# State parts by pairs, a searched order, and one transposing transfer per chunk in place of TensorE turns

## The chip, the cores and the metric

The kernel runs on one core of a Trainium2 chip. The metric is the device time of one execution in microseconds. The engines are TensorE (PE, with its weight loads as PEld), VectorE (DVE), ScalarE (ACT), GpSimd (POOL) and SyncE (SP), which only issues transfers.

## The reference

A gated linear attention over 4 batches, 8 heads, 768 tokens and heads of 48 is followed by a token and channel mixer. In NumPy, cut to what matters:

```python
f = 1.0 / (1.0 + np.exp(-f_logit))
for t in range(S):                       # state: (B, H, 48, 48)
    state = f[:, :, t, :, None] * state + einsum('bhd,bhe->bhde', k[:, :, t], v[:, :, t])
    y[:, :, t] = einsum('bhd,bhde->bhe', q[:, :, t], state)
x = y.transpose(0, 2, 1, 3).reshape(B, S, 384)
h = maximum(x.transpose(0, 2, 1) @ w_tok1, 0) @ w_tok2     # 768 -> 256 -> 768
u = x + h.transpose(0, 2, 1)
out = u + maximum(u @ w_ch1, 0) @ w_ch2                    # 384 -> 1536 -> 384
```

## The kernel before

Each batch is cut into 6 chunks of 128 tokens. For a chunk, `gates` computes the log of the gate in three ACT ops and splits it into two bfloat16 parts, `Lhi` and `Llo`. `attention` then does the following, with buffer set `i = c % 2`:

- `sums` (L350 to L353): PE sums the logs over tokens with a triangular matrix, and over the whole chunk with a vector of ones.
- ACT takes the exponentials `G` and `Gi` (L361, L363) and, for all but the last chunk, `glast` (L366). DVE makes `qh = q*G` and `kh = k*Gi` (L369, L371), each padded to 64 columns per head.
- `turn` (L382): PE transposes `qh` and `kh`, four 128x128 blocks each, into one PSUM bank; DVE copies the bank to `qkT` (L386).
- `scores` (L396): for each head a product with 48 rows on one half of the array's rows; DVE masks both banks into `AmT` (L403).
- `parts` (L419): for each head the chunk's state update from `kh` and `v`, 64 columns of the array wide, two heads of a pair one above the other in one bank. DVE adds it to the state (`tsum`, L429) and scales by `glast` (L431; chunk 0 does both in L426). ACT, or POOL in batch 3, copies the state in two halves into `state_bd`.
- `outs` (L448, L455): PE multiplies `qkT` by the state before this chunk and `AmT` by `v` into one bank, which is copied to `x_bf` and `x_nat` (L311 on ACT, L313 on DVE; ACT alone in batch 0).

`mixer` follows for each batch: tok1 (L480), tok2 (L492) with the add L496 and the copy to `u_bf` (L311), transposes (L508) to `uT` (L513), ch1 (L524) with a relu on ACT (L534) or DVE (L536), ch2 (L546) with the add L552, and the store on SP's queue (L555). Loads of weights and of q, k, v go through POOL's queue (L255, L262); the first six gate loads go through SP's.

The order is not the program's. Every step is recorded with `add`: the engines that may run it, a rank, the buffers it needs and makes, its PSUM bank and a `kind` from which `Plan.cost` has its time. `Plan.order` keeps a clock for each engine and takes, again and again, the step that can start first, with the rank deciding between equals; it also picks the engine where several are allowed, and the PSUM bank. The steps are issued in the order of their planned starts, so each engine's queue is fixed before the kernel runs, and an engine waits at the head of its queue. The lines that say the choice:

```python
t = max(t, free[e])
if op.bank is not None and op.bank.at is None:
    t = max(t, min(banks) + 55)
if best is None or (t, op.rank) < best[0]:
    best = ((t, op.rank), e, op)
```

Ranks come from due times: attention of batch 0 every 3 us a chunk, of batch 1 from 36 us every 4, of later batches from 62 us and 101 us every 5, so that attention of one batch runs between the ch1 and ch2 products of the batch before it.

Of the kernel before, what the change touches and what calls it, by code (L numbers as in the profile page):

```python
# [10 lines left out]
FP32 = mybir.dt.float32  # L11
BF16 = mybir.dt.bfloat16
# [5 lines left out]
NBANK = 8  # L18
RING = 16384

# [19 lines left out]
class Plan:  # L40
# [58 lines left out]
    def order(self):  # L99
        for op in self.ops:  # L100
            first = op.before | ({op.behind} if op.behind else set())
            op.missing = len(first)
            for x in first:
                x.after.append(op)
        free = {e: 0.0 for e in (PE, ACT, DVE, POOL, SP)}
        ready = {e: [] for e in free}
        banks = [0.0] * NBANK
        wire = 0.0
        landed: list = []
        done = []  # L110

        def offer(op):
            t = max([x.end for x in op.before], default=0.0)
            if op.kind[0] == "load" and op.engines == (POOL,) and op.kind[3]:
                if len(landed) >= 8:
                    t = max(t, landed[-8][0])
                held = op.kind[2]
                for at, rows in reversed(landed):
                    held += rows
                    if held > RING:  # L120
                        t = max(t, at)
                        break
            for e in op.engines:
                ready[e].append((t + (WAKE[e] if t else 0.0), op))

        for op in self.ops:
            if not op.missing:
                offer(op)
        while len(done) < len(self.ops):
            best = None  # L130
            for e, line in ready.items():
                for t, op in line:
                    if op.engine is not None:
                        continue
                    t = max(t, free[e])
                    if op.bank is not None and op.bank.at is None:
                        t = max(t, min(banks) + 55)
                    if best is None or (t, op.rank) < best[0]:
                        best = ((t, op.rank), e, op)
            (t, _), e, op = best  # L140
            ready[e] = [(a, o) for a, o in ready[e] if o is not op and o.engine is None]
            if op.bank is not None and op.bank.at is None:
                op.bank.at = min(range(NBANK), key=lambda j: banks[j])
                banks[op.bank.at] = math.inf
            own, till = self.cost(op, e)
            op.engine, op.start = e, t
            free[e] = t + own
            op.end = t + till
            if op.kind[0] == "load":
                size = op.kind[3]  # L150
                if size:
                    wire = max(wire, t + 1700) + size
                    op.end = wire + 1100
                if size and e == POOL:
                    landed.append((op.end, op.kind[2]))
            if op.bank is not None:
                op.bank.users -= 1
                if not op.bank.users:
                    banks[op.bank.at] = op.end
            done.append(op)  # L160
            for x in op.after:
                x.missing -= 1
                if not x.missing:
                    offer(x)
        return sorted(done, key=lambda o: o.start)
# [7 lines left out]
def kernel(  # L173
# [20 lines left out]
    NB = 3  # L194

# [22 lines left out]
    G = [st([128, H, D], BF16, f"G{i}") for i in range(2)]  # L218
    Gi = [st([128, H, D], BF16, f"Gi{i}") for i in range(2)]
    qh = [st([128, H, 64], BF16, f"qh{i}") for i in range(2)]  # L220
    kh = [st([128, H, 64], BF16, f"kh{i}") for i in range(2)]
    qkT = [st([128, 8, 128], BF16, f"qkT{i}") for i in range(2)]
    AmT = [st([128, 8, 128], BF16, f"AmT{i}") for i in range(2)]
    glast = [st([128, HP], FP32, f"glast{i}") for i in range(2)]
    state = st([128, HP, D], FP32, "state")
    tsum = st([128, HP, D], FP32, "tsum")
    state_bd = [st([128, HP, 2 * D], BF16, f"state_bd{i}") for i in range(2)]
# [54 lines left out]
    for i in range(2):  # L282
        for n, tl in (("L", Lhi[i]), ("L", Llo[i])):
            once(DVE, lambda tl=tl: nc.vector.memset(tl[:, :, :, D:64], 0.0), [("L", i, c) for c in range(NCH)], 400)
        for n, tl in (("qh", qh[i]), ("kh", kh[i])):
            once(DVE, lambda tl=tl: nc.vector.memset(tl[:, :, D:64], 0.0), [(n, i)], 120)
        once(DVE, lambda i=i: nc.vector.memset(state_bd[i], 0.0), [("sbd", i)], 220)
# [47 lines left out]
    def attention(b, c, r):  # L335
        i, nb = c % 2, b % NB
# [43 lines left out]
        def turn(src, o):  # L380
# [3 lines left out]
        add(PE, r, lambda: turn(qh[i], 0), need=["ident", ("qh", i)], bank=p_t, kind=mms(*[C] * 4))  # L384
        add(PE, r, lambda: turn(kh[i], 4), need=["ident", ("kh", i)], bank=p_t, kind=mms(*[C] * 4))
        add(DVE, r, lambda: nc.vector.tensor_copy(qkT[i], turned()), make=[("qkT", i)], bank=p_t,  # L386
            kind=("el", 1024, True, 2))
# [11 lines left out]
        add(PE, r, lambda: None, need=[("qkT", i)], bank=p_a[0], kind=("mm", 1))  # L399
        two = add(PE, r, scores, need=[("qkT", i)], bank=p_a[1], kind=("mm", 270))  # L400
# [9 lines left out]
        if not last:  # L410
            p_d = Bank()

            def dg():
                return banks[p_d.at][:, 0:HP * D].rearrange("p (hp e) -> p hp e", e=D)

            def parts():
                for h in range(H):
                    hp, par = h // 2, h % 2
                    nc.tensor.matmul(dg()[par * 64:par * 64 + 64, hp, :], lhsT=kh[i][:, h, :],  # L419
                                     rhs=v_sb[nb][:, h, c, :], start=True, stop=True)  # L420

            add(PE, r, parts, need=[("kh", i), vk], bank=p_d, kind=("mm", 210))
            gb = glast[i].unsqueeze(2).broadcast_to((128, HP, D))
            small = ("el", HP * D, True, 1)
            if c == 0:
                add(DVE, r, lambda: nc.vector.tensor_tensor(state, dg(), gb, ALU.mult),  # L426
                    need=[("glast", i)], make=["state"], bank=p_d, kind=small)
            else:
                add(DVE, r, lambda: nc.vector.tensor_tensor(tsum, state, dg(), ALU.add),  # L429
                    need=["state"], make=["tsum"], bank=p_d, kind=small)  # L430
                add(DVE, r, lambda: nc.vector.tensor_tensor(state, tsum, gb, ALU.mult),  # L431
                    need=["tsum", ("glast", i)], make=["state"], kind=small)
            for rows, cols in ((slice(0, D), slice(0, D)), (slice(64, 64 + D), slice(D, 2 * D))):
                op = add(ACT if b <= 2 else POOL, r, None, need=["state"], make=[("sbd", i, cols.start)],
# [10 lines left out]
        def before():  # L445
            yh = y().rearrange("t (h e) -> t h e", e=D)
            for hp in range(HP):
                nc.tensor.matmul(yh[:, 2 * hp:2 * hp + 2, :], lhsT=qkT[i][:, hp, :],  # L448
                                 rhs=state_bd[(c - 1) % 2][:, hp, :],
# [10 lines left out]
        j = (c - 1) % 2  # L460
# [6 lines left out]
        past = [("qkT", i), ("sbd", j), ("sbd", j, 0), ("sbd", j, D)] if c > 0 else []  # L467
        add(PE, r, outs, need=[*past, ("AmT", i, 0), ("AmT", i, 1), vk], bank=p_y,
            kind=mms(*([96] * 4 if c else []), *[48] * 8))
        for tl, key in ((x_bf[b % 2], ("x_bf", b % 2, c)), (x_nat[b % 3], ("x_nat", b % 3, c))):  # L470
            op = add(ACT if b == 0 else (ACT, DVE), r, None, make=[key], bank=p_y, kind=el)
# [144 lines left out]
```

## Time and profile before

| what | us |
|---|---|
| median of 3 runs (188.82 to 189.28) | 188.99 |
| the profiled execution, its own time | 188.64 |
| its span | 186.8 |
| first PE instruction | 6.08 |
| first ch1 product of batch 0 | 37.75 |
| end of the last ch2 product | 183.4 |

The span is the time from the first to the last instruction of the program; 1.84 us of the execution lie around it. Busy shares over the span are PE 92%, DVE 69%, ACT 68% and POOL 35%. A PE instruction's listed time includes its way through the array, and the next one starts before it ends, so what a group costs PE is the time from its start to the next group's start. The same holds for DVE and ACT, whose ops overlap by some 0.08 to 0.12 us.

### The profile page before, as it was taken

What the parts mean: (1) busy time and instruction counts of PE and PEld (TensorE: products, weight loads), DVE (VectorE), ACT (ScalarE), POOL (GpSimd) and SP (SyncE); (2) the same over time, 40 slices, a digit from 0 to 9 for tenths busy, and PEclk for the clock granted to TensorE, in tenths of its full rate; (3) what the DMA queues carried; (4) which work ended last, traced back from release to release, by engine and by line L of the source; (5) the groups of instructions that cost most, each with busy time, mean ns of one, the idle gap of its engine ahead of it and who ended that gap; (6) DMA issues with size and microseconds to landing.
All of it is one profiled execution on the core that took longest, in us unless ns stands there. A gap on an engine that the chain in (4) does not pass through costs nothing.

```text
span 186.8 us, 4480 instructions
## 1 busy us (share of the span) xinstructions
PE 172.5 (92%) x1768; PEld 109.6 (59%) x1768; DVE 129.7 (69%) x295; ACT 126.9 (68%) x309; POOL 65.9 (35%) x78
## 2 busy tenths in 40 slices
PE   0589997799999999999999999999999999999992
PEld 0256664366667656676665665766666656656650
DVE  4387985749998999999988758977686638300222
ACT  4779963779983499999999935657875116698000
POOL 7999893275791444504621411011011000000000
PEclk9999999999999999999999999999999999999998
DMA  7999999999999999999992121011000121110222
GB/s 102 140 171 154 156 208 245 186 160 194 143 135 238 174 149 172 242 200 109 83 116 14 52 78 42 0 46 44 4 0 4 55 75 40 46 42 0 81 91 84
DMA packets 88437, 19.95 MB, mean 107 GB/s; under 512 B 81152, under 2 KB 87600, under 8 KB 88416
## 3 DMA queue, kind: packets, MB, share of 16 engines
q0 software_dynamic: 78720, 13.77, 91.9%
q1 hardware_dynamic: 9696, 5.90, 10.8%
q8 instruction: 14, 0.23, 0.5%
q14 instruction: 7, 0.06, 0.1%
HBM read 25.17 MB, written 4.72 MB: 160 GB/s over the span
## 4 chain that ended last, share of the span: by engine, by line
PE 84%; ACT 6%; DVE 3%; issue 2%; DMA 2%; POOL 1%; POOLq 0%; DVEq 0%; ACTq 0%
PE ps L524 26%; PE ps L546 24%; PE ps L382 7%; PE ps L480 5%; PE ps L396 4%; PE ps L492 3%; PE ps L455 3%; PE ps L419 3%; PE ps L352 2%; PE ps L508 2%; PE ps L353 2%; DMA f_sb<-in_f_logit_dram 2%; PE ps L448 2%; ACT u_bf L311 2%; ACT x_bf L311 1%
## 5 line engine op out<-in xcount | busy, mean ns | idle before, releaser
L546 PE MATMUL ps<-w_ch,zT 128*128 128x384 bf16 x288 | 54.1, 327 | 0.0
L524 PE MATMUL ps<-uT,w_ch 128*128 128x384 bf16 x288 | 52.6, 327 | 0.0
L534 ACT ACTIVATE zT<-ps 128x384 bf16<-128x384 f32 x76 | 36.5, 490 | 8.3 <-PE ps L524 7.9
L546 PEld LDWEIGHTS <-zT 128*128 128x128 bf16 x288 | 26.8, 98 | 16.5
L524 PEld LDWEIGHTS <-w_ch 128*128 128x128 bf16 x288 | 26.3, 97 | 15.9
L403 DVE TENSOR_TENSOR AmT<-ps,tri_bf 128x512 bf16<-128x512 f32 x48 | 30.6, 683 | 5.2 <-PE ps L396 5.0
L552 DVE TENSOR_TENSOR x_nat<-x_nat,ps 128x384 f32<-128x384 f32 x24 | 13.2, 550 | 22.9 <-PE ps L546 22.5
L255 POOL DMA_DIRECT2D q_sb<-in_q_dram x14 | 15.4, 1099 | 13.8 <-issue 5.7
L311 ACT ACTIVATE x_bf<-ps 128x384 bf16<-128x384 f32 x20 | 9.9, 494 | 12.9 <-PE ps L455 12.7
L255 POOL DMA_DIRECT2D k_sb<-in_k_dram x14 | 15.5, 1108 | 7.6 <-DMA f_sb<-in_f_logit_dram 4.5
L361 ACT ACTIVATE G<-ps 128x384 bf16<-128x384 f32 x24 | 11.7, 488 | 7.9 <-PE ps L353 7.8
L386 DVE COPY qkT<-ps 128x1024 bf16<-128x1024 bf16 x24 | 16.4, 685 | 0.8 <-PE ps L382 0.7
L255 POOL DMA_DIRECT2D v_sb<-in_v_dram x14 | 15.5, 1104 | 4.1 <-issue 2.5
L496 DVE TENSOR_TENSOR x_nat<-x_nat,ps 128x384 f32<-128x384 f32 x24 | 11.5, 548 | 4.1 <-PE ps L492 4.1
L311 ACT ACTIVATE u_bf<-x_nat 128x384 bf16<-128x384 f32 x24 | 11.4, 523 | 4.1 <-DVE x_nat L496 4.1
L315 POOL CAST state_bd<-state 48x192 bf16<-48x192 f32 x10 | 3.4, 343 | 29.8 <-DVE state L431 24.3
L324 ACT ACTIVATE f_sb<-f_sb 128x384 f32<-128x384 f32 x24 | 12.0, 523 | 2.7 <-DMA f_sb<-in_f_logit_dram 2.6
L480 PE MATMUL ps<-x_bf,w_tok 128*128 128x384 bf16 x48 | 12.3, 340 | 1.0 <-ACT x_bf L311 1.0
L536 DVE TENSOR_SCALAR zT<-ps 128x384 bf16<-128x384 f32 x20 | 10.4, 553 | 3.7 <-PE ps L524 3.6
L311 ACT ACTIVATE state_bd<-state 48x192 bf16<-48x192 f32 x30 | 10.8, 360 | 2.9 <-DVE state L431 2.6
L350 PE MATMUL ps<-ones_bf,Lhi 128*128 128x1 bf16 x80 | 7.0, 167 | 6.1 <-ACT Lhi L326 6.1
L326 ACT ACTIVATE Lhi<-f_sb 128x384 bf16<-128x384 f32 x24 | 12.2, 522 | 0.3
(58 smaller groups left out, 276.3 us busy)
## 6 DMA issues: line engine op xcount, KB each, us to landing
out_dram<-x_nat SPq DMA_DIRECT2D x24, 192.0 KB, 1.9
f_sb<-in_f_logit_dram POOLq DMA_DIRECT2D x3, 1152.0 KB, 11.0
f_sb<-in_f_logit_dram SPq DMA_DIRECT2D x6, 192.0 KB, 4.0
k_sb<-in_k_dram POOLq DMA_DIRECT2D x12, 96.0 KB, 6.3
q_sb<-in_q_dram POOLq DMA_DIRECT2D x12, 96.0 KB, 5.9
v_sb<-in_v_dram POOLq DMA_DIRECT2D x12, 96.0 KB, 6.0
w_ch<-in_moe_w_ch_dram POOLq DMA_DIRECT2D x2, 576.0 KB, 11.0
w_ch<-in_moe_w_ch_dram POOLq DMA_DIRECT2D x1, 1152.0 KB, 14.6
```

The lines of the kernel that those rows point to most:

```text
L255: add(engine, 0.0, lambda eng=eng, into=into, of=of: eng.dma_start(out=into, in_=of), make=[(n, b % NB, j) for j in (range(NCH) if c is No ...
L311: nc.scalar.activation(out_, in_, AF.Copy, bias=0.0, scale=1.0)
L324: add(ACT, r, lambda: nc.scalar.activation(fb, fb, AF.Exp, bias=0.0, scale=-1.0), make=[key], kind=el)
L326: add(ACT, r, lambda: nc.scalar.activation(hi, fb, AF.Copy, bias=0.0, scale=1.0), need=[key], make=[lk], kind=el)
L382: nc.tensor.transpose(turned()[:, o + hp, :], blk(src)[:, hp, :], ident)
L386: add(DVE, r, lambda: nc.vector.tensor_copy(qkT[i], turned()), make=[("qkT", i)], bank=p_t, kind=("el", 1024, True, 2))
L403: add(DVE, r, lambda p=p: nc.vector.tensor_tensor(AmT[i][:, 4 * p:4 * p + 4, :], banks[p_a[p].at].rearrange("s (hp t) -> s hp t", t=C), tb ...
L480: add(PE, rank("tok1", rt), lambda rt=rt, kt=kt, pm=pm: nc.tensor.matmul(banks[pm.at][:, 0:DM], lhsT=w_tok1[:, kt, rt * 128:(rt + 1) * 128 ...
L524: nc.tensor.matmul(banks[pm.at][:, 0:384], lhsT=w[:, kt, c0:c0 + 128], rhs=uT[:, kt, cols], start=(kt == 0), stop=(kt == 2))
L534: nc.scalar.activation(zT[:, cc, cols], banks[pm.at][:, 0:384], AF.Relu, bias=0.0, scale=1.0)
L546: nc.tensor.matmul(banks[pm.at][:, 0:DM], lhsT=zT[:, kt, tt * 128:(tt + 1) * 128], rhs=w_ch2[:, kt, :], start=(kt == 0), stop=(kt == 11))
L552: add(DVE, rank("ch2", tt), lambda un=un, pm=pm: nc.vector.tensor_tensor(un, un, banks[pm.at][:, 0:DM], ALU.add), make=[("x_nat", xn, tt)] ...
```

## The change

It has three parts and some small ones.

- **State parts.** In batches 1 to 3 `parts` makes four products of 128 columns by 96 for pairs of heads in place of eight of 64 by 48. The bank then holds four 48x48 blocks a pair, of which the two on the diagonal are used, so the DVE op that reads the bank is cut in two, by halves of the partitions. Batch 0 keeps the old form (`BYHEAD`).
- **Copies and plan.** In batch 0 the copy to `qkT` is cut in two halves that DVE or ACT may run (`SPLIT`), and its copies to `x_bf` and `x_nat` may run on DVE too. Three buffer sets for chunks replace two (`NI`). The planner's pass becomes `attempt`; it adds a cost where PE changes the array's shape (`TURN`), slows PE by 1.9 before 28 us (`COLD`), and reads its ranks from a list. `order` starts from the ranks given, then shifts a share of the ranks at random 600 times and keeps each result that the plan's own clock finds no later. (`slack` is defined and not called.)
- **Turning.** In batch 3 (`MOVED`) no transposes are made on PE and no copy on DVE: SP issues one transposing transfer per chunk from `qkh`, which holds `qh` and `kh` side by side, to `qkT`.

The diff, cut to its core:

```diff
+TURN = 105
+COLD = 28000
+TRIES = 600
...
-    def order(self):
+    def attempt(self, rank):
...
+            if e == PE:
+                way = op.kind[2] if len(op.kind) > 2 else ""
+                if op.kind[1] > 1:
+                    if way != mode:
+                        t = max(t, free[PE] + TURN)
+                    mode = way
...
+            if e == PE and t < COLD:
+                own, till = 1.9 * own, 1.9 * own + 180
...
+    def order(self):
...
+        rank = [o.rank for o in self.ops]
+        found = self.attempt(rank)
+        rank, rnd = list(found[1]), random.Random(1)
+        for _ in range(TRIES):
+            far, share = rnd.choice((300, 1000, 3000)), rnd.choice((0.02, 0.1, 0.5))
+            other = [r + (rnd.gauss(0, far) if rnd.random() < share else 0) for r in rank]
+            now = self.attempt(other)
+            if now[0] <= found[0]:
+                found, rank = now, other
...
+    NI = 3
+    SPLIT = (0,)
+    BYHEAD = (0,)
+    MOVED = (3,)
...
+    qkh = [st([128, 2 * H, 64], BF16, f"qkh{i}") for i in range(NI)]
+    qh = [t[:, 0:H, :] for t in qkh]
+    kh = [t[:, H:2 * H, :] for t in qkh]
...
-        i, nb = c % 2, b % NB
+        i, nb = (b * NCH + c) % NI, b % NB
...
-        add(PE, r, lambda: turn(qh[i], 0), need=["ident", ("qh", i)], bank=p_t, kind=mms(*[C] * 4))
-        add(PE, r, lambda: turn(kh[i], 4), need=["ident", ("kh", i)], bank=p_t, kind=mms(*[C] * 4))
-        add(DVE, r, lambda: nc.vector.tensor_copy(qkT[i], turned()), make=[("qkT", i)], bank=p_t,
-            kind=("el", 1024, True, 2))
+        if b in MOVED:
+            add(SP, r, lambda: nc.sync.dma_start_transpose(qkT[i], qkh[i].rearrange("t n d -> t (n d)")),
+                need=[("qh", i), ("kh", i)], make=[("qkT", i, 0), ("qkT", i, 4)], kind=("fix", 1000, 4000))
+        else:
+            add(PE, r, lambda: turn(qh[i], 0), need=["ident", ("qh", i)], bank=p_t, kind=mms(*[C] * 4))
+            add(PE, r, lambda: turn(kh[i], 4), need=["ident", ("kh", i)], bank=p_t, kind=mms(*[C] * 4))
+            for o in (slice(0, 4), slice(4, 8)) if b in SPLIT else (slice(0, 8),):
+                op = add((DVE, ACT) if b in SPLIT else DVE, r, None,
+                         make=[("qkT", i, x) for x in (0, 4) if o.start <= x < o.stop], bank=p_t,
+                         kind=("el", (o.stop - o.start) * C, True, 2))
+                op.fn = lambda op=op, o=o: copy_on(op.engine, qkT[i][:, o, :], turned()[:, o, :])
...
             def parts():
...
+                dg2 = banks[p_d.at][:, 0:DM].rearrange("p (h e) -> p h e", e=D)
+                for hp in range(HP):
+                    nc.tensor.matmul(dg2[:, 2 * hp:2 * hp + 2, :], lhsT=blk(kh[i])[:, hp, :],
+                                     rhs=v_sb[nb][:, 2 * hp:2 * hp + 2, c, :], start=True, stop=True)
...
+            for rows, cols, at in [both] if b in BYHEAD else halves:
+                if c == 0:
+                    add(DVE, r, lambda rows=rows, cols=cols: nc.vector.tensor_tensor(
+                        state[rows], dg(rows, cols), gb[rows], ALU.mult),
...
+                else:
+                    add(DVE, r, lambda rows=rows, cols=cols: nc.vector.tensor_tensor(
+                        tsum[rows], state[rows], dg(rows, cols), ALU.add),
...
-            op = add(ACT if b == 0 else (ACT, DVE), r, None, make=[key], bank=p_y, kind=el)
+            op = add((ACT, DVE), r, None, make=[key], bank=p_y, kind=el)
```

## The prediction

> **What bounds the kernel now.** I read the page's first lines and its row of slices, then windows of busy time cut where TensorE (PE) changes character, then the timeline inside the long stretch for the price of one instruction group. The page first:
>
> ```profile
> span 186.8 us, 4480 instructions
> PE 172.5 (92%) x1768; PEld 109.6 (59%) x1768; DVE 129.7 (69%) x295; ACT 126.9 (68%) x309; POOL 65.9 (35%) x78
> ...
> DVE  4387985749998999999988758977686638300222
> ACT  4779963779983499999999935657875116698000
> ```
>
> PE is busy 92% of the span, but VectorE (DVE) and ScalarE (ACT) are also at 9 tenths in many of the 40 slices before the middle. The windows separate the stages; the columns after the length are PE, weight loads, DVE, ACT and POOL busy:
>
> ```profile
> 6.08:28.68 22.60, 20.32 (x228) 13.37 (x229) 17.99 (x42) 18.29 (x49) 21.93 (x27) 1.00 1.96 171
> 28.68:37.75 9.07, 6.90 (x71) 3.98 (x70) 6.24 (x14) 5.46 (x12) 1.91 (x3) 1.00 1.40 213
> 37.75:183.40 145.65, 145.26 (x1474) 92.23 (x1470) 102.65 (x230) 99.80 (x243) 37.19 (x36) 1.00 0.89 90
> ```
>
> From 37.75 us (the first ch1 product of batch 0) to 183.40 us PE has work in 145.26 of 145.65 us: whatever PE no longer does there comes off the end. Before 37.75 us, PE idles 2.28 + 2.17 = 4.45 us, in a chain over all engines. After 183.40 us come the last add and store, 3.4 us, untouched. Busy time of PE is pipelined, so the price of a group is from its start to the start of the next one. The timeline has every group that the change touches:
>
> ```profile
> 98.90 0.40 PE L382 MATMUL ps<-ident,qh 128*128 128x128 bf16 x4
> 99.23 0.31 PE L419 MATMUL ps<-v_sb,kh 128*64 128x48 bf16 x8
> 99.47 0.66 PE L524 MATMUL ps<-uT,w_ch 128*128 128x384 bf16 x3
> 99.97 0.39 PE L382 MATMUL ps<-ident,kh 128*128 128x128 bf16 x4
> 100.19 0.81 PE L546 MATMUL ps<-w_ch,zT 128*128 128x384 bf16 x4
> ...
> 103.55 0.33 PE L448 MATMUL ps<-state_bd,qkT 128*128 128x96 bf16 x4
> 103.72 0.36 PE L455 MATMUL ps<-v_sb,AmT 128*128 128x48 bf16 x8
> ```
>
> Four transposes before an ordinary product take 0.22 us (99.97 to 100.19); before the state parts, which use half the columns of the array, 0.33 (98.90 to 99.23). So PE pays about 0.09 us to enter that shape; over all 15 such groups the entry is 91 to 94 ns. The parts themselves take 0.24 us. Four products of 128x96 on the whole array take 0.17 us (103.55 to 103.72).
>
> **The change part by part.**
>
> State parts by pairs, batches 1 to 3, 5 chunks each: 15 groups of 0.241 + 0.093 = 0.334 us become 15 of four 128x96 products, 0.170 us. That is 0.164 x 15 = 2.46 us less on PE, all inside the dense stretch. The price is on DVE: the two useful halves of the result lie in different columns, so each op that reads it is cut in two by partitions. Per batch that adds one op in chunk 0 and one in each of chunks 1 to 4, so 15 ops in all. Their length is set by the 192 elements, not the partitions; its price is read here:
>
> ```profile
> 53.19 0.34 DVE L429 TENSOR_TENSOR tsum<-state,ps 128x192 f32<-128x192 f32 x1
> 53.45 0.55 DVE L329 TENSOR_TENSOR Llo<-f_sb,Lhi 128x384 bf16<-128x384 f32 x1
> ...
> 54.18 0.69 DVE L386 COPY qkT<-ps 128x1024 bf16<-128x1024 bf16 x1
> ```
>
> 53.19 to 53.45 is 0.26 us, so 15 ops are some 4 us of DVE, ten of them in batches 1 and 2.
>
> Transfer in place of turning, batch 3: 6 chunks lose 8 transposes each, 8 x 56 ns = 0.447 us (twice the 0.22 above), together 2.68 us of PE in the dense stretch, and 6 copies of 0.60 us (54.18 to DVE's next start, 54.78). Three transposes of batch 0's mixer (L508) stand behind the first ch1 products in the new order, 0.17 us into the stretch. So the dense stretch loses 2.46 + 2.68 - 0.17 = 5.0 us, if nothing makes PE wait. As a check I added the new PE order group by group with these prices: from the first ch1 product to the end it comes to 139.1 us; the old order's stretch less 5.0 is 140.6 with its stalls.
>
> What covers the transfer is the distance, in that order, from a chunk's column sums to its scores: 8.2, 10.9, 9.6, 6.5, 6.9 and 8.6 us of PE work for the six chunks. Of it, sums to finished kh took 2.65 us around 101 us (sums end 101.33, kh ends 103.98), which leaves 3.8 us for the tightest chunk. The trace has no transfer of this kind: 256 KB, on-chip at both ends. The nearest rows:
>
> ```profile
> out_dram<-x_nat SPq DMA_DIRECT2D x24, 192.0 KB, 1.9
> ...
> f_sb<-in_f_logit_dram SPq DMA_DIRECT2D x6, 192.0 KB, 4.0
> k_sb<-in_k_dram POOLq DMA_DIRECT2D x12, 96.0 KB, 6.3
> ```
>
> The store is nearest: same queue, and it runs in the same quiet stretch (DMA engines 0 to 2 tenths busy after 98 us, 9 tenths when the other two ran). I take 3 us, so no stall, with 1.9 and 6.3 as ends; without cover every microsecond beyond 3.8 reaches PE, which takes its queue in order. On SP's queue, two transfers stand before stores of batch 1; a store held there costs nothing, since batch 1's x_nat buffer is not written again. A transfer in turn waits for at most the sixth ch2 result of batch 1, which in the new PE order is complete 1.7 us of PE work before the third chunk's sums end; so none is late for that.
>
> [...]
>
> Batch 0's stage, before 37.75 us: the qkT copy is cut in two halves, one on each of DVE and ACT, the x copies may go to either engine, three buffer sets replace two, and the order is searched. PE runs here at half pace until about 28.5 us, by its own rows: four transposes at 11.80 us took 0.54 us against 0.22 later, a group of scores 0.54 us at 28.00 and 0.33 at 29.02. The most to be won is the 4.45 us of idle PE. The most to be lost is ACT's extra load, six half copies of about 0.5 us less four x copies of 0.39, 1.4 us. The copy of 0.69 us becomes two side by side, an estimated 0.42 us on DVE (between its rows of 0.35 for 384 and 0.69 for 1024 columns) and 0.6 on ACT (0.49 for 384, scaled to 512). That is worth between 6 x 0.1 = 0.6 us (the later half ends sooner) and 6 x 0.27 = 1.6 (what DVE is relieved of, 0.60 less some 0.33); I take 0.8, since PE's wait for qkT in this stage is 1.9 us in three places. The order also has 18 changes of array shape here in place of 21, 0.09 to 0.19 us each by pace, 0.4. I take 1.2 us, with -1.4 and 4.4 as ends. Three more memsets on DVE (0.44 us) lie in its 2.8 us of idle before the first Llo.
>
> DVE, the second engine: between the last tok2 add (L496) of batch 0 and that of batch 1, 36.6 to 79.8 us, the old DVE order holds ops worth 37.8 us at their start-to-start prices, the new one 43.2 (halves, more relus, more of batch 2 pulled ahead). The new stretch, by the PE order up to batch 1's last tok2 product, is about 44 us, so DVE goes from 87% to 98% of it. In the old trace PE stalls 0.31 and 0.26 us at 67 us behind a full DVE. I take another 0.6; the ends are 0 and 5.4, all that DVE gained.
>
> Sum, against the profiled execution: 188.64 - 5.0 - 1.2 + 0.6 = 183.0. The median of the runs is 0.35 above that execution, so 183.4 us.
>
> **The rivals.**
>
> (a) DVE becomes the bound in batches 1 and 2. For: 98% leaves no room for a wait. Against: DVE idles little today and PE has ch1 and ch2 products to fill with. At its worst the 5.4 us come back: 188.64 - 5.0 - 1.2 + 5.4 = 187.8, 188.2 at the median; halfway, 185.8.
>
> (b) The transfers are slow and follow one another on SP's queue. With the first ch1 product at 36.55 us, the first chunk's sums end 70.0 us of PE work later, so its transfer starts at 106.6 + 2.65 = 109.2; the last chunk's scores are due 104.6 us of PE work after that product, at 141.2. Six transfers of x us end at 109.2 + 6x, a delay of 6x - 32.0. It outweighs the gain of 5.6 from x = 6.3 us on, which is the slow load's row: 189.2 there. At 11.0 us, the median of a 576 KB weight load, the delay is 34.0 and the time 188.99 - 5.6 + 34.0 = 217.4. For it: no row shows an on-chip transfer that turns its data. Against: the store row, and idle DMA engines.
>
> (c) Batch 0's stage gains nothing or loses its 1.4: 184.6 to 186.0 at the median.
>
> **How the numbers follow.** The forecast has 0.68, (a) 0.12, (b) 0.11, (c) 0.09. A measurement here tells apart about 0.3%, 188.4 to 189.6. (a) and (c) end faster, (a)'s far end only just; (b) is slower from 6.4 us on and no change around 6.3. So faster 0.86, same 0.04, slower 0.10. The low end, 180.9, is 188.99 - 5.0 with 3.1 us won in batch 0's stage and no stall on DVE; the high end, 187.4, takes in (c) and most of (a) and leaves out (b).
>
> **What would show it.** Right: the PE window from the first ch1 product to the end is 140 to 141.5 us, with PE busy throughout; of the 20 half-array groups of parts 5 are left, in batch 0; the transfers take 2 to 4 us from issue to landing; the first ch1 product starts near 36.5 us. Wrong: PE waits for qkT ahead of batch 3's scores between 110 and 145 us (then b); PE waits for DVE between 40 and 80 us with DVE without a gap (then a); the first ch1 product after 37.75 (then c).

## The result, and the profile after

The changed kernel takes 190.51 us, the median of 11 runs (189.49 to 191.44), beside 188.96 for the kernel before on the same chip (11 runs). The ratio is 1.0082, with a 95% interval of 1.0057 to 1.0107. It is slower, where 183.4 was forecast. The profiled execution takes 189.81 us with a span of 188.0. First its page: the two lines of totals, the slices of DVE and ACT, and the shares of the chain that ended last.

```profile
span 188.0 us, 4278 instructions
PE 168.4 (90%) x1660; PEld 106.6 (57%) x1660; DVE 137.0 (73%) x318; ACT 123.0 (65%) x304; POOL 65.9 (35%) x78
...
DVE  5278889699999999999999766698688647400222
ACT  4699955689783789899999413387874126697000
...
PE 50%; DVE 20%; ACT 20%; issue 4%; DMA 2%; POOL 1%; POOLq 0%; DVEq 0%; ACTq 0%
```

PE has 108 instructions and 4.1 us of busy time less, and the kernel is no faster for it: PE fell from 92% to 90% of a longer span. DVE gained 7.3 us and is at 9 tenths in 14 slices in a row. In the page of before the same line of shares had PE at 84%, ACT at 6 and DVE at 3; now the chain runs through DVE and ACT for 40%. The windows, cut where those of before were (the last column group is clock, DMA share, GB/s; the clock's record begins at 27.43 us, so the 1.00 of the first row says nothing of the pace before it):

```profile
5.68:27.43 21.75, 17.61 (x205) 11.87 (x206) 15.46 (x37) 18.02 (x48) 21.33 (x27) 1.00 1.97 168
27.43:38.92 11.49, 8.22 (x93) 4.78 (x92) 9.24 (x22) 7.61 (x18) 3.60 (x5) 1.00 1.51 202
38.92:183.80 144.88, 142.27 (x1368) 89.97 (x1365) 108.73 (x245) 94.08 (x236) 36.47 (x36) 1.00 0.95 100
```

Two sizes tell the story, and every kernel below is read by them. **The first ch1 product** starts at 38.92 us in place of 37.75; 36.55 was forecast. **The dense stretch**, from there to the start of the last ch2 product, is 144.88 us; before it was 145.18 (37.75 to 182.93; that product ends at 183.26), and 140.8 was forecast (145.18 - 5.0 + 0.6). So 2.4 of the 6.8 us that the profiled execution lies above the forecast's 183.0 are in batch 0's stage, 4.1 in the dense stretch and 0.3 behind it. The time between PE's products that neither streaming nor a change of shape explains, summed over the dense stretch, went up by some 4.6 us, from about 2.1 to 6.7, and nearly all of it lies between 50 and 110 us. Without it the stretch is some 143.1 us before and 138.2 after: PE's work did go down by about the forecast 5 us, and waits took it back.

The transfers are what was hoped: 3.1 us in the list of DMA issues, and no PE wait for `qkT` in batch 3. The second fence is the tile's summary, with SP's own time for the issue in ns.

```profile
qkT<-qkh SPq DMA_TRANSPOSE x6, 3.1
```

```profile
L451 SPq DMA_TRANSPOSE qkT<-qkh x6: 1232/1235/1349, 117.0 to 144.6; - x6
...
DMA to landing us min/median/max: 3.0/3.1/4.2
```

Two things in the trace were not foreseen. In the timeline of DVE, the two half ops of a pair (`tsum`, 64 partitions, x2) keep the engine from 67.86 to 68.60, 0.74 us, where the one op of before kept it for 0.26:

```profile
66.66 1.28 DVE L477 TENSOR_TENSOR AmT<-ps,tri_bf 128x512 bf16<-128x512 f32 x2
67.86 0.71 DVE L518 TENSOR_TENSOR tsum<-state,ps 64x192 f32<-64x192 f32 x2
68.60 0.56 DVE L395 TENSOR_TENSOR Llo<-f_sb,Lhi 128x384 bf16<-128x384 f32 x1
```

And in batch 0 the chain of waits has the two halves of the copy to `qkT` one behind the other, first DVE's, then ACT's, 1.06 us from 12.20 to 13.26, where one DVE op of 1024 columns took 0.69. In the trace ACT's half waits for the semaphore that DVE's half sets:

```profile
12.20 0.44 DVE qkT L379
12.66 0.60 ACT qkT L377
```

### The profile page after: what moved, and what is told of

It reads as the page before. It is cut to its first block, busy times and chain, and to the rows that moved or that the text cites. A ratio compares the mean times of both kernels' runs of the same rounds, so it can differ in the third digit from the quotient of the medians.

```text
span 188.0 us, 4278 instructions
## 1 busy us (share of the span) xinstructions
PE 168.4 (90%) x1660; PEld 106.6 (57%) x1660; DVE 137.0 (73%) x318; ACT 123.0 (65%) x304; POOL 65.9 (35%) x78
## 4 chain that ended last, share of the span: by engine, by line
PE 50%; DVE 20%; ACT 20%; issue 4%; DMA 2%; POOL 1%; POOLq 0%; DVEq 0%; ACTq 0%
PE ps L637 20%; PE ps L615 17%; DVE AmT L477 7%; ACT state_bd L377 3%; ACT u_bf L377 3%; DVE qkT L379 3%; PE ps L571 2%; PE ps L583 2%; ACT zT L625 2%; ACT Lhi L392 2%; DMA f_sb<-in_f_logit_dram 2%; ACT f_sb L390 2%; ACT f_sb L391 2%; DVE Llo L395 2%; PE ps L599 2%
## 5 line engine op out<-in xcount | busy, mean ns | idle before, releaser
L637 PE MATMUL ps<-w_ch,zT 128*128 128x384 bf16 x288 | 53.4, 326 | 0.0
L625 ACT ACTIVATE zT<-ps 128x384 bf16<-128x384 f32 x68 | 31.7, 492 | 7.3 <-PE ps L615 6.9
L615 PEld LDWEIGHTS <-w_ch 128*128 128x128 bf16 x288 | 26.8, 98 | 16.7 <-issue 0.8
L448 PE MATMUL ps<-ident,qkh 128*128 128x128 bf16 x144 | 15.9, 247 | 3.5 <-DVE qkh L435 2.3
L377 ACT ACTIVATE x_nat<-ps 128x384 f32<-128x384 f32 x13 | 6.3, 488 | 15.7 <-DVE x_bf L379 13.5
L448 PEld LDWEIGHTS <-qkh 128*128 128x128 bf16 x144 | 11.0, 110 | 8.1 <-DVE qkh L435 4.0
L627 DVE TENSOR_SCALAR zT<-ps 128x384 bf16<-128x384 f32 x28 | 14.6, 551 | 1.1 <-PE ps L615 0.9
L587 DVE TENSOR_TENSOR x_nat<-x_nat,ps 128x384 f32<-128x384 f32 x24 | 11.5, 545 | 3.5 <-PE ps L583 3.5
L571 PE MATMUL ps<-x_bf,w_tok 128*128 128x384 bf16 x48 | 12.8, 331 | 0.2 <-ACT x_bf L377 0.2
L395 DVE TENSOR_TENSOR Llo<-f_sb,Lhi 128x384 bf16<-128x384 f32 x18 | 9.8, 553 | 3.7 <-ACT Lhi L392 3.4
```

Source lines behind the costliest of these rows:

```text
L377: nc.scalar.activation(out_, in_, AF.Copy, bias=0.0, scale=1.0)
L395: add(DVE, r, lambda: nc.vector.tensor_tensor(lo, fb, hi, ALU.subtract), need=[key], make=[lk], kind=el)
L448: nc.tensor.transpose(turned()[:, o + hp, :], blk(src)[:, hp, :], ident)
L571: add(PE, rank("tok1", rt), lambda rt=rt, kt=kt, pm=pm: nc.tensor.matmul(banks[pm.at][:, 0:DM], lhsT=w_tok1[:, kt, rt * 128:(rt + 1) * 128 ...
L615: nc.tensor.matmul(banks[pm.at][:, 0:384], lhsT=w[:, kt, c0:c0 + 128], rhs=uT[:, kt, cols], start=(kt == 0), stop=(kt == 2))
L625: nc.scalar.activation(zT[:, cc, cols], banks[pm.at][:, 0:384], AF.Relu, bias=0.0, scale=1.0)
```

## Experiments

All ratios are to the kernel before, run on the same chip, which had medians of 188.6 to 189.2 us. Kernels that are said to keep an order have every engine's instructions in that order except where the edit takes one out, puts one in or puts one in another's place. The edits are told in short, not as the program's lines. Eight of the eighteen runs came out slower than every range that was expected for them.

**One op in place of two halves, in the changed kernel's order.** Its state parts keep the order; both halves become one op.

```diff
-for rows, cols, at in halves: tsum[rows] = state[rows] + dg(rows, cols)
+rows = slice(0, 128)                     # one op, cols of the even heads
```

> The changed kernel with the same order on every engine, but each of the 15 pairs of half ops on the state parts is one op over all 128 partitions that reads the first half's columns (the odd heads' state parts are left out). Theory 1, DVE is the bound between 40 and 104 us and the half ops are what fills it: 15 ops fewer, 4 to 6 us of DVE freed, PE's stalls between 40 and 104 us (5.2 us now beyond changes of array shape) fall under 2 and the time to 185.5 to 188. Theory 2, what was lost is batch 0's stage alone (first ch1 product at 38.9 us) and the searched order as such: within 0.5 us of the changed kernel's 190.5. Theory 3, the transfers hold PE up: no change either.

Measured: 188.74 us (187.95 to 189.21), ratio 0.9992 (0.9964 to 1.0019). The dense stretch is 143.27 us, 1.6 shorter, and the first ch1 product stays at 38.86. So the halves explain 1.8 of the 7.1 us that the result lies above the forecast.

**Two ops, but without the change of partitions.**

```diff
-second half: tsum[64:128] = state[64:128] + dg(64:128)
+second half: spare[0:64] = state[0:64] + dg(0:64)
```

> The changed kernel with the same order and the same number of DVE ops, but the second op of each pair works on partitions 0 to 63 again and writes a spare tile (the odd heads' state is left out). In the changed kernel the second half starts 0.35 to 0.39 us after the first, not 0.27, and the op behind it often too. Theory 1a, it is the move to other partitions that holds an op until the one before has ended: the pairs go at 0.27 us, 2 to 3 us of DVE are freed, the time falls by 0.7 to 2 us. Theory 1b, the number of ops alone counts: within 0.5 us of 190.5.

Measured: 189.27 us (188.20 to 189.77), ratio 1.0011 (0.9981 to 1.0041): 1.2 below the changed kernel, 0.5 above one op. So more of the 1.8 comes with the change of partitions than with the second op itself, though the smaller step is near what these medians can tell apart. In the timeline of DVE the two ops now keep the engine for 0.53 us, where the halves of the changed kernel kept it for 0.74:

```profile
68.64 0.33 DVE L523 TENSOR_TENSOR tsum<-state,ps 64x192 f32<-64x192 f32 x1
68.90 0.34 DVE L523 TENSOR_TENSOR spare<-state,ps 64x192 f32<-64x192 f32 x1
69.17 0.54 DVE L396 TENSOR_TENSOR Llo<-f_sb,Lhi 128x384 bf16<-128x384 f32 x1
```

Its dense stretch is 143.1 us, as short as with one op: in the stretch the second op by itself cost nothing that shows. But its first ch1 product starts at 40.56 us, with the same order of every engine. The record of the granted clock has full pace from 34.2 us on in this execution, and from 27.4 and 27.8 in those of the changed kernel and of one op. So the first ch1 product of a single trace can differ by 1.7 us with nothing changed in front of it, and smaller differences of it, the 1.2 us of the changed kernel among them, are to be read with that in mind.

**The search left out.**

```diff
-TRIES = 600
+TRIES = 0
```

> The changed kernel without the search: the order is the planner's first pass with the ranks given. Theory 2, the searched order is fragile in batch 0's stage, where ACT has the gate of chunk 2 ahead of G of chunk 0 and waits 1.5 us for its load: the first ch1 product is back at 37.8 us or earlier and the time is 188 to 189.5. Theory 1: DVE still has 15 ops more, so PE stalls 3 us or more between 40 and 104 us and the time is 189 to 192.

Measured: 193.15 us (193.05 to 193.98), ratio 1.0256 (1.0209 to 1.0304); first ch1 product 41.05. The search wins 2.6 us over its own start. Without it the first ch1 product comes later, not earlier. It mends an order that starts out worse than before's.

**Parts by head in all batches, searched anew.**

```diff
-BYHEAD = (0,)
+BYHEAD = (0, 1, 2, 3)
```

> The changed kernel with the old state parts by head in all batches, the search run anew. Theory 1: 2.5 us more of PE work but 15 DVE ops fewer; DVE is no longer the bound and the time is 186 to 188.5. If PE set the pace as the prediction had it, the 2.5 us would come on top: 192.5 to 193.5.

Measured: 191.90 us (191.06 to 193.09), ratio 1.0185 (1.0124 to 1.0246); first ch1 product 40.22. A new search gives another order, so this run does not price the pairs: batch 0, which the edit does not touch, moved by 1.3 us, and the clock fell back to half pace from 26.3 to 33.1 us. This is why the later runs keep an order.

**Each part alone, with the planner of before.** The transfer in batch 3:

```diff
-turn(qh), turn(kh), copy to qkT         # batch 3
+nc.sync.dma_start_transpose(qkT[i], qkh[i])
```

> The kernel before with the transfers of batch 3 alone: first planner without search, two buffer sets, parts by head, batch 0 as before. The order is the same as before's up to mixer 2. The transfer is a real gain (PE 2.7 us less in a stretch that PE bounds, landing in 3 to 4 us as in the changed kernel): 186 to 186.8. The transfer costs as much as it saves, through late scores or copies that were hidden: 188.5 to 189.5.

Measured: 186.27 us (186.00 to 186.57), ratio 0.9851 (0.9819 to 0.9883). The dense stretch is 142.28 us, 2.90 shorter, where 2.68 was forecast for this part. It beats both kernels.

The pairs in batches 1 to 3:

```diff
-parts: eight products 64 columns by 48, one DVE op
+parts: four products 128 by 96, two DVE ops on 64 partitions
```

> The kernel before with parts by pairs in batches 1 to 3 alone, first planner, no search. PE has 2.5 us less to do, DVE 15 ops more, 0.27 to 0.39 us each. If DVE had room: 186.3 to 187. If DVE is as good as the bound between 40 and 104 us: 188.5 to 191, PE's stalls there rising from 2 us to 5 or more.

Measured: 192.22 us (191.16 to 192.97), ratio 1.0162 (1.0118 to 1.0207), where 186.5 would be the forecast of this part alone. First ch1 product 37.58; the stretch is 148.72.

Three buffer sets and the free copies of batch 0:

```diff
+NI = 3; SPLIT = (0,); x copies on ACT or DVE in batch 0
```

> The kernel before with three buffer sets, the qkT copy of batch 0 in two halves on DVE or ACT and its x copies on either, first planner, no search. Theory 2b, these are what made batch 0's stage longer: the first ch1 product comes at 38.5 to 41 us in place of 37.75 and the time is 189.8 to 193. If they help as meant: first ch1 product by 37 us, 187.5 to 188.5.

Measured: 197.74 us (197.24 to 198.75), ratio 1.0465 (1.0424 to 1.0506); first ch1 product 42.61.

All three with the planner of before:

```diff
-TURN = 105; COLD = 28000; TRIES = 600; two.before.add(one)
+TURN = 0; COLD = 0; TRIES = 0
```

> The changed kernel's three parts ordered by the planner of before: no price for a change of array shape, no slow PE before 28 us, no search, and scores that do not wait in the plan for the step that claims their first bank. Theory 2c, the new planner's clock made the order worse (its first pass gave 193.15): 186 to 189.5. If the parts themselves are what costs: 190.5 to 193.

Measured: 194.55 us (193.97 to 194.66), ratio 1.0284 (1.0254 to 1.0313); first ch1 product 44.0. The new planner is worth 4.0 us to the three parts together, and batch 0's stage, which ends 5.1 us earlier with it (38.92), is more than all of that.

**What of the sets and the split.**

```diff
+SPLIT = (0,); x copies on ACT or DVE in batch 0       # split_only
+NI = 3                                                # sets_only
```

> The kernel before, with the copy to qkT in batch 0 cut in two halves that DVE or ACT may run and the x copies free for either engine; two buffer sets, first planner. Theory: the two halves read one bank and run one after the other, 1.05 us in place of 0.69, and the planner, which has them side by side, builds an order on it; the array then falls back to half pace. Then the first ch1 product starts 2 to 5 us later than 37.75 and the time is 191 to 194, and more of the 8.8 us that the split and the third set cost together is here. Rival: the third buffer set is what costs; then this is 188.5 to 190.

> The kernel before with three buffer sets for chunks in place of two, nothing else. The order of PE differs from before's only late in the third batch. Theory that the split does the harm: 188.5 to 189.5. Rival, that the third set lets attention run ahead and fill DVE at the wrong time: over 190.

Measured: the split 196.98 us (196.35 to 197.74), ratio 1.0435 (1.0377 to 1.0493), first ch1 product 43.33; the sets 189.41 (188.30 to 191.14), ratio 1.0037 (0.9998 to 1.0077), first ch1 product 37.90. The harm comes from the split together with the free x copies, which no run parts: six of batch 0's twelve x copies move to DVE, which (in the trace that has the three sets as well) waits 2.8 us for ACT's copies out of the same banks, and PE waits 2.4 us there for the halves of `qkT`, the most for any tile after its first product. The chain of waits shows the same pairs in either order of engines, each begun when the other has ended:

```profile
11.10 0.44 DVE qkT L378
11.56 0.61 ACT qkT L376
...
25.16 0.60 ACT qkT L376
25.79 0.42 DVE qkT L378
```

Slower products then add to the delay. In the timeline of PE the twelve tok2 products of batch 0 take 3.9 us at 37.82, from first to last start 3.53; in before it was 2.01:

```profile
36.92 0.49 PE L569 MATMUL ps<-x_bf,w_tok 128*128 128x384 bf16 x2 [0.58 <-ACT x_bf L376]
37.82 3.91 PE L581 MATMUL ps<-h1T,w_tok 128*128 128x384 bf16 x12 [0.42 <-ACT h1T L573]
41.56 0.72 PE L597 MATMUL ps<-ident,u_bf 128*128 128x128 bf16 x10
```

The granted clock of that run is at full pace from 31.2 to 38.0 us and at half from 38.0 to 41.4, after a stage in which PE kept waiting (2.9 us in five waits, between 33.2 and 37.8 us).

**The split joined again, in the changed kernel's order.**

```diff
-first half on DVE or ACT, second half on DVE or ACT
+nothing; one DVE copy of 1024 columns, where the later half stood
```

> The changed kernel, its order kept, but in batch 0 the copy to qkT is one DVE op of 1024 columns, at the place of the later half, in place of two halves on DVE and ACT. Theory that the halves run one after the other on one bank, 1.05 us against 0.69, and cost batch 0's stage: the first ch1 product moves from 38.9 to 37 to 38, and the time from 190.5 to 188.6 to 189.8. Rival, that batch 0's stage is late for the gate that ACT has in front of G, or for the order at large: no change, 190 to 191.

Measured: 190.18 us (189.31 to 190.64), ratio 1.0053 (1.0028 to 1.0079); first ch1 product 39.81. The time lies in the range of the rival, but the run is inconclusive. At the later place the joined copy stands behind other DVE work, and PE waits 1.6 us for it at 23.30, once: the edit made a new wait that is longer than what it could save there. In its trace the clock is also at half pace from 24.5 to 34.8 us, where the changed kernel's is at full pace from 27.4.

**The new planner alone, without the three parts.**

```diff
+attempt, TURN, COLD, search; NI = 2, SPLIT = (), BYHEAD all, MOVED = ()
```

> The kernel before with the planner of the changed one (change of shape, half pace, 600 shifted rank lists), two buffer sets, none of the three parts. If the search is worth what it was in the changed kernel (193.15 without it, 190.5 with it), and the start is as good as before's order: 186.5 to 189. If the new costs and the step that scores must wait for make the start worse, as in the changed kernel without the search: 189 to 192.

Measured: 191.65 us (191.21 to 192.07), ratio 1.0129 (1.0095 to 1.0162). The windows of this run:

```profile
27.89:36.57 8.68, 6.67 (x72) 4.01 (x72) 5.95 (x14) 5.71 (x13) 3.15 (x4) 1.00 1.22 222
36.57:185.50 148.93, 144.96 (x1472) 92.82 (x1470) 104.77 (x234) 96.83 (x238) 37.20 (x36) 1.00 0.89 88
```

Without the split the new planner's batch 0 does end at 36.57 us, where the forecast had it. But its dense stretch is 148.93 us, 3.75 longer than before's with the same work on PE. PE's listed waits there come to 3.7 us: 2.4 for `qkh`, 0.9 for `qkT` and 0.4 for a load of `v`. One place of it, in the timeline:

```profile
67.67 0.56 DVE L378 CAST x_bf<-ps 128x384 bf16<-128x384 f32 x1 [2.06 <-ACT x_nat L376]
68.14 0.68 DVE L378 COPY qkT<-ps 128x1024 bf16<-128x1024 bf16 x1
...
68.88 0.40 PE L468 MATMUL ps<-qkT 48*128 48x128 bf16 x8 [0.90 <-DVE qkT L378]
```

DVE stands 2.06 us behind ACT's copy out of the same bank, `qkT` comes late, and PE waits 0.90 us. The planner lets two engines read one bank together; in the trace one waits for the other. That is one place: in sum DVE waits 5.1 us for ACT's copies out of the same bank in this stretch, and 5.7 in before, so such waits as a whole do not explain the 3.75 us.

**Pairs with one op, in the order made for pairs.**

```diff
-for rows, cols, at in halves: ...         # of the run with pairs alone
+rows = slice(0, 128)
```

> Pairs alone with the first planner, as in the run with pairs alone, with the order of every engine kept, but the bank of a pair is read by one DVE op on 128 partitions where two on 64 were; the state parts of odd heads are left out. The pairs take 15 x 0.164 = 2.46 us from PE, and the run with pairs alone was 192.2 against 188.95. If the halves (15 ops more, and the time for which the second is held) are all of that loss: 186.5. If the order that the planner makes of the pairs is what costs (ops of DVE placed by a clock that has no price for waits of this sort, and other relus on DVE): it stays above 190.3, of which the halves explain the 1.8 us that the same edit was worth in the changed kernel. In between, both.

Measured: 190.26 us (188.57 to 191.60), ratio 1.0062 (1.0021 to 1.0103). The halves are worth 2.0 us here as well, and the order made for the pairs keeps it 1.4 above before.

**Pairs in the order of before.** The plan goes on costing them as the old form; only what is issued changes.

```diff
+add(DVE, r, joined, ...)                  # one step of the plan issues both halves
-kind=mms(*[2 * D] * 4)
+kind=("mm", 210, "col")
```

> The kernel before with its order of every engine kept, and in it the 15 groups of parts of batches 1 to 3 made by pairs, each read by two DVE ops one right behind the other. The plan goes on costing them as the old form. Theory that the pairs' own price is small and the re-planning around them costs: 188.9 - 2.46 = 186.5, plus what the second halves cost where DVE is full, ten in batches 1 and 2 at 0.35 us, 0 to 3.5: 186.5 to 188.4. Rival, that the held halves alone undo the gain: 189 to 191, as in the two runs with pairs alone (192.2, and 190.3 with one op).

> The run with pairs in the kept order (193.5), with the same order of every engine, but each pair's bank read by one DVE op on 128 partitions; the state parts of odd heads are left out. In that run a pair's two halves keep DVE for 0.35 + 0.39 = 0.74 us where the one op kept it for 0.26, or 0.82 for 0.46 ahead of the op that needs it: 6.6 us over 15 pairs, and 189.2 - 2.46 + 6.6 = 193.3. If the held halves are all: 186.5 to 187. If something else of the pairs costs (their products on PE, the wait for the bank): it stays over 188.5.

Measured: with halves 193.53 us (193.18 to 193.72), ratio 1.0226 (1.0195 to 1.0257), with one op 187.56 (185.93 to 187.82), ratio 0.9930 (0.9901 to 0.9959). The stretches are 149.47 and 143.87 us, so in a fixed order the halves alone cost 5.6 us, and pairs without them win 1.3 of the 2.46. DVE of the first run around 62 us:

```profile
61.90 0.69 DVE L378 COPY qkT<-ps 128x1024 bf16<-128x1024 bf16 x1
62.51 0.71 DVE L517 TENSOR_TENSOR tsum<-state,ps 64x192 f32<-64x192 f32 x2
63.25 0.56 DVE L644 TENSOR_TENSOR x_nat<-x_nat,ps 128x384 f32<-128x384 f32 x1
63.72 0.68 DVE L378 COPY qkT<-ps 128x1024 bf16<-128x1024 bf16 x1
...
64.46 0.23 PE L468 MATMUL ps<-qkT 48*128 48x128 bf16 x2 [0.78 <-DVE qkT L378]
```

and of the second:

```profile
60.63 0.34 DVE L517 TENSOR_TENSOR tsum<-state,ps 128x192 f32<-128x192 f32 x1
60.90 0.55 DVE L644 TENSOR_TENSOR x_nat<-x_nat,ps 128x384 f32<-128x384 f32 x1
61.36 0.68 DVE L378 COPY qkT<-ps 128x1024 bf16<-128x1024 bf16 x1
```

From `tsum` to the op behind it is 0.74 us in the first and 0.27 in the second, the copy to `qkT` follows later by the same amount, and PE's scores wait for that copy. Summed over the 15 pairs, the starts of one run against those of before give 6.6 us of DVE: 4.6 in batches 1 and 2, 2.0 in batch 3.

**Both savings together in a kept order.**

```diff
+dma_start_transpose in batch 3, and the pairs of the run above in batches 1 to 3   # move_pairs_kept
+the same with pairs in batch 3 only                                                # move_pairs3_kept
```

> The kernel with the transfer in batch 3 alone (186.3), its order kept, and in it the parts by pairs as in the run with pairs in the kept order. If both savings stand in an order that is not made anew: 186.3 - 2.46 = 183.8, to 185.7 with held halves. If the pairs' gain is lost to DVE in the kept order too: 186.3 to 188.

> The kernel with the transfer in batch 3 alone (186.3), its order kept, with the parts by pairs in batch 3 only, where DVE is far from full and has no copy to qkT behind the halves. By the theory of held halves their 2.0 us of DVE are covered there and 5 x 0.164 = 0.8 us of PE come off: 185.3 to 185.9. If the halves reach PE here too, by the state or by the masked scores behind them: 186.3 to 187.

Measured: with all pairs 189.17 us (187.25 to 189.83), ratio 0.9984 (0.9954 to 1.0014); with those of batch 3 only 185.39 (184.93 to 185.78), ratio 0.9818 (0.9782 to 0.9853). The window of the second, over its dense stretch:

```profile
38.31:179.82 141.51, 141.25 (x1404) 89.67 (x1402) 100.76 (x229) 98.45 (x242) 37.19 (x36) 1.00 0.97 103
```

With all pairs, the halves in batches 1 and 2 give the transfer's whole gain back. The best stretch, 141.51 us, is 0.77 less than with the transfer alone, against 5 x 0.164 = 0.82 forecast, and PE is busy throughout (one trace of each). Where DVE had room (33.8 of 46.0 us busy between 104 and 150 us in the trace of before), and no copy to `qkT` stood behind the halves, the pairs were worth what PE's rows say. The intervals of the two ratios overlap, so between these two it is the trace that shows it. This is the best version that was run.

**The transfer in batch 2 as well.**

```diff
-MOVED = (3,)
+MOVED = (2, 3)                            # otherwise as the transfer alone
```

> The kernel before with the transposing transfer in batches 2 and 3, nothing else. It takes 12 x 0.447 = 5.4 us from PE and 12 copies of 0.60 us from DVE, six of them in the stretch in which DVE is nearly full. If the transfers of batch 2 land in 3 to 4 us as those of batch 3 did (6 of them, alone 186.3): 183.6. If the loads on the DMA engines up to 98 us slow them to the 6 to 11 us that loads take there, with two buffer sets in turn: PE waits for qkT in batch 2, and the time is 186 to 189.

Measured: 195.28 us (194.56 to 196.81), ratio 1.0352 (1.0269 to 1.0435). SP's timeline has three transfers between 77 and 94 us; the tile's summary for 76 to 104 us gives issue to landing; and PE waits for the first of them:

```profile
77.81 15.89 SPq L450 DMA_TRANSPOSE qkT<-qkh  x3
```

```profile
DMA to landing us min/median/max: 6.6/8.1/11.5
```

```profile
81.55 0.66 PE L597 MATMUL ps<-ident,u_bf 128*128 128x128 bf16 x9
89.39 0.61 PE L468 MATMUL ps<-qkT 48*128 48x128 bf16 x8 [7.18 <-DMA qkT<-qkh]
```

Beside the loads (168 GB/s from 76 to 98 us) the same transfer takes 6.6 to 11.5 us in place of 3.1, as the loads' own rows had it; the seven that the same run issues from 106.7 us on land in 3.0 to 4.5. PE lies idle for 7.2 us, and the granted clock is at half pace from 86.6 to 93.4.

## Why the prediction was wrong

**Right.** PE's prices: the pairs' 0.164 us each show in the best version (0.77 us for five), and the transfer alone took 2.90 us off the stretch for 2.68. The transfer's 3 us met 3.1, with 4.2 at the longest, so rival (b) is out for batch 3; the reason given for the store's row, quiet DMA engines, is borne out by the transfers in batch 2, which met the slow loads' row (6.6 to 11.5 us).

**Wrong: the price of the halves.** The step "53.19 to 53.45 is 0.26 us, so 15 ops are some 4 us" took the row of an op whose neighbours work on the same partitions. Two halves keep DVE for 0.35 + 0.39 us in place of 0.26, so the second op costs 0.48, not 0.26, and ten of them in batches 1 and 2 cost 4.6 us. One op is as long as the prediction had it, 0.35 us on 64 partitions as on 128, but the halves do not overlap: in the trace of the pairs in the kept order each second half begins 13 to 32 ns after the first one's end, and the op behind it 31 to 35 ns after that in ten of the 15 pairs, 104 to 134 in the five others; other ops mostly begin 80 to 85 ns before the last one's end. With both ops on the same partitions the second began at 68.90 us, some 70 ns before the end of the first (68.64 and 0.33 us).

**Wrong: the 0.6 us for DVE.** Rival (a), at 0.12, is in part what happened in the dense stretch: one op in place of two halves gave back 1.6 of its 4.1 us. DVE was put at 98% of its stretch, and a tenth of what it gained was charged to PE. In a fixed order the halves' 6.6 us of DVE became 5.6 us of time. Without them the pairs win 1.3 of 2.46 us: in that trace PE's listed waits for DVE in the stretch come to 0.9 us, where before has none, and the rest is not shown. The prediction itself says that 98% "leaves no room for a wait", and then takes a number that has room for one.

**Wrong: the order as a neutral carrier.** The prediction costed the new order as if it had only the stalls of the old. From before's 145.18 us, the transfer's 2.9 and 1.3 for pairs with one op go off and the 1.6 of the halves in the changed kernel's order comes on: 142.6. The changed kernel has 144.88, so some 2.3 us are left for the new order. That remainder is a subtraction, and no run isolates it; but the new planner alone lengthened the same work by 3.75 us. Its clock knows neither a held op (0.74 us for two halves, 0.53 on the same partitions), nor that two engines take turns at one bank (1.06 us for the halves of the copy), and it makes each scores step wait in the plan for a step that issues nothing. The first two hold for the clock of before as well, so which term of the new planner does the harm stays open. One wait of 0.77 us in the changed kernel's stretch has another source, shown at the end.

**Wrong: batch 0's stage.** The step "two side by side" failed. The halves of the copy read one PSUM bank, and DVE and ACT took turns: 1.06 us in place of 0.69, where 0.6 was assumed for the later half. In all six chunks of batch 0 in the changed kernel's trace the second half began only after the first had ended, 31 to 109 ns after it in five and 747 in one. Before's list of waits already had the evidence, 5.7 us in 12 waits of DVE's `x_nat` copy for ACT's `x_bf` copy of the same bank:

```profile
DVE x_nat L313 <- ACT x_bf L311: 5.7, 12, 0.9
```

The prediction's 1.9 us of PE waiting for `qkT` are the row of PE's weight loads; its products wait for 0.8 us, once. The first ch1 product stands at 38.9 us or later in every kernel with the split and the free x copies (38.86 to 44.0), and at 36.6 to 38.5 in all without. With the first planner the two move it from 37.75 to 43.33. In the changed kernel the split's share of the 2.4 us is not isolated, since the joined copy made a wait of its own. Its trace has more than one cause: in that stage PE waits 1.7 us for the halves of `qkT`, and 2.6 us for `qkh` (0.6 for `qh` before). The longest of these waits, 1.8 us, comes from the order: ACT has two gate ops of a later chunk, and the wait for their load, in front of the first chunk's `G`, where before has one such op; `G` starts at 9.13 us in place of 8.06:

```profile
8.14 0.52 ACT L390 ACTIVATE f_sb<-f_sb 128x384 f32<-128x384 f32 x1 [1.55 <-DMA f_sb<-in_f_logit_dram]
...
9.13 0.47 ACT L427 ACTIVATE G<-ps 128x384 bf16<-128x384 f32 x1
...
9.63 0.36 DVE L435 TENSOR_TENSOR qkh<-q_sb,G 128x384 bf16<-128x384 bf16 x1 [2.45 <-ACT G L427]
```

So parts of rivals (a) and (c) came together with a cost of the new order that no rival had, and the prediction had priced each rival alone.

## What to carry to other kernels

Before work is moved from the engine that is busiest to the one that is second, price the new ops by rows in which their neighbours are like their new neighbours (same partitions, same bank), and count the whole of it as time where the second engine is as full as DVE was here (50.6 of 54.0 us between 44 and 98 us). To see what a change is worth under a planner that makes the order anew, first put it into the old order by hand; here that gave the best version, with the transfer where the DMA engines were quiet and the pairs only where DVE had room. A transfer that was quick in a quiet stretch (3.1 us in batch 3) has to be priced again for each stretch into which it is moved (6.6 to 11.5 us in batch 2).

## What the hardware showed beyond that

Two of DVE's products to `qkh`, usually 0.35 us, took 0.76 and 0.87 us beside an op of POOL in the changed kernel's timeline, and PE waited for the second:

```profile
102.15 0.91 POOL L398 TENSOR_TENSOR Llo<-f_sb,Lhi 128x384 bf16<-128x384 f32 x1 [1.88 <-ACT Lhi L392]
102.40 0.87 DVE L437 TENSOR_TENSOR qkh<-k_sb,Gi 128x384 bf16<-128x384 bf16 x1
103.20 0.68 DVE L477 TENSOR_TENSOR AmT<-ps,tri_bf 128x512 bf16<-128x512 f32 x1
103.33 0.34 PE L497 MATMUL ps<-v_sb,qkh 128*128 128x96 bf16 x4 [0.77 <-DVE qkh L437]
```

One product each took 0.78, 0.78 and 0.99 us beside the same op of POOL in the runs with one op, with two ops on the same partitions and with the planner alone; in before one that ran beside it took 0.35. No run isolates this. The granted clock also fell back to half pace after it had opened: for 3.4 us in the kernel with the split alone, for 6.8 us around the idle 7.2 us of the kernel with the transfer in batch 2, and within batch 0's stage of several others, the transfer alone (22.7 to 29.5 us) and the pairs in the kept order (19.9 to 30.1) among them. In the first two it went with PE's waits (2.9 us in five, and 7.2 us in one), and the products behind them were slower: 3.53 us in place of 2.01 for the twelve of tok2, and 0.61 for the first eight of the scores, which took 0.40 in before at 29.02 us. So a late buffer cost its delay and the slower products behind it; no run isolates the fall of the clock.
